# Pairing score units 13 to 20 and issuing one weight load ahead of a cast, in a fused attention and gated-MLP kernel

## Chip, cores and metric

The kernel runs on one core of a Trainium2 chip. The metric is the device time of one execution in microseconds (us). A core has a tensor engine (PE), a vector engine (DVE), a scalar engine (ACT), a Pool engine (POOL) and a sync engine (SP). Each works through its own instruction list in order, and they meet at semaphores. DMA transfers are issued here by SP, ACT and POOL and carried out by 16 DMA engines.

## What is computed

```python
# q: (8, 16, 384, 64)   k, v: (8, 4, 384, 64), each k/v head serves four q heads
scores = scale * np.matmul(q, k.transpose(0, 1, 3, 2))
attn = np.exp(scores - np.max(scores, axis=-1, keepdims=True))
attn = attn / (np.sum(attn, axis=-1, keepdims=True) + 1e-09)
x = np.matmul(attn, v)               # heads side by side: (8, 384, 1024)
h = np.maximum(x @ w_in, 0.0)        # w_in: (1024, 1024)
u, v = h[..., :512], h[..., 512:]
v_n = (v - mean(v)) / np.sqrt(var(v) + 1e-06)
v_s = np.einsum('ts,bsd->btd', w_spatial, v_n) + b_spatial[None, :, None]
out = (u * v_s) @ w_out              # w_out: (512, 1024)
```

## The kernel before

**Work and its pieces.** There are eight batches. The attention of a batch is cut into six sets (three blocks of 128 queries by two groups of heads), and a set into three units, one for each block of 128 keys. So a batch is 18 units and the whole kernel 144. For a unit, `units` (its matmuls on line 278) makes two score tiles of 128x512, called sc, one for each head half (hh 0 and 1); these two matmuls use 64 rows of the array each and start together. `exp` (line 290) turns each into a part of aT on ACT. When the three units of a set are done, `weigh` (line 298) multiplies aT with v, once per head half, in 12 matmuls of 65 columns into av; DVE divides by the row sums (lines 311 and 313) and writes x. `x_turn`, `q_turn` and `k_turn` transpose x, q and k on PE (tiles xps, qps, kps), and DVE copies them out of PSUM (line 216). From the second batch on, x is transposed by DMA (`x_send`, line 337), and from the third on so are k and q (`k_send`, line 248, and `q_send`, line 256).

**The gated part.** `v_part` (line 353) multiplies the transposed x with the v half of w_in, in eight matmuls per block of 128 rows into one PSUM bank (pv). DVE then applies the maximum (line 367) and the statistics (line 379). `u_part` (412), `s_part` (431) and `o_part` (469) make u, the spatial product and the output. A generator, `gated`, hands out these matmuls one by one.

**Order.** The order is written out by hand and is the program's order on every engine. For units 0 to 20 the loop takes one unit at a time: the unit's two scores and its exponentials, then what the table `todo` puts there (casts, transposes, loads), then the halves of `weigh` that are due, then `pour` takes gated matmuls out of the generator until a budget of 736 ns, less 224 for a transpose and 372 for a half of `weigh`, is spent. From unit 21 on the loop takes the three units of a set together, six scores in a row. `bank` gives each PSUM tile one of eight banks by a planner's clock of its own.

**Start.** The v half of w_in comes in two transfers on POOL's queue, `load_w_in(1, 0, 4)` and `load_w_in(1, 4, 8)` (line 161), each 512 rows of 512 float32 columns, cast to float16 on the way. `v_part` needs the first for its matmuls 0 to 3 and the second for 4 to 7. POOL also casts k, v and part of q (lines 185, 189, 206), and SP brings the rest of batch 0's q (`rest_q`, two transfers on line 122). In front of the scores of batch 1 stand `k_turn(1, 0)` at unit 15, `q_turn(1, 0, 0)` at unit 16, `k_turn(1, 1)` and `q_turn(1, 1, 0)` at unit 18; `x_turn` stands at units 5, 9, 12, 15, 18 and 21.

Of the kernel before, what the change touches and what calls it, by code (L numbers as in the profile page):

```python
# [17 lines left out]
def kernel(  # L18
# [58 lines left out]
    def bank(shape, dtype, name):  # L77
        i = min(range(8), key=done.__getitem__)
        t = ps.tile(shape, dtype, name=name, tag=f"bank{i}")
        clock[nc.tensor] = max(clock[nc.tensor], done[i])  # L80
        done[i] = 1e12 + clock[nc.tensor]
        taken[name] = i
        return t

    def spend(ns):
        clock[nc.tensor] += ns

    def reads(eng, ns, name=None):
        clock[eng] = max(clock[eng], clock[nc.tensor] + 200.0) + ns
        if name:  # L90
            done[taken.pop(name)] = clock[eng]
# [67 lines left out]
    def load_w_in(half, lo, hi):  # L159
        cols = slice(half * DH, (half + 1) * DH)  # L160
        pool.dma_start(
            w_in16[:, lo:hi, cols],
            moe_w_in[lo * P : hi * P, cols].rearrange("(t p) f -> p t f", p=P),
        )
# [22 lines left out]
    def cast_v(b, eng, js=(0, 1)):  # L187
        g0, g1 = 2 * js[0], 2 * js[-1] + 2
        eng.tensor_copy(
            v1[b % 2][:, g0:g1, :, 0:D].rearrange("p g t d -> p (g t) d"),  # L190
            stage["v", b, None][:, g0:g1].rearrange("p g (t d) -> p (g t) d", t=NT),
        )

    def cast_q(b, j, eng, ts=None, hs=(0, 1)):
        if (b, j) not in q16s:
            q16s[b, j] = ld.tile([P, NT, G, 2, D], FP16, name=f"q16_{b}_{j}", tag="q16", bufs=4)
        t16 = q16s[b, j]
        src = stage["q", b, j].rearrange("p h t (r d) -> p h t r d", d=D)
        for hh in hs:
            if ts is None:  # L200
                eng.tensor_copy(t16[:, :, :, hh, :], src[:, hh])  # L201
            elif len(ts) > 1:
                t = slice(ts[0], ts[-1] + 1)
                eng.tensor_copy(t16[:, t, :, hh, :], src[:, hh, t])  # L204
            else:
                eng.tensor_copy(t16[:, ts[0], :, hh, :], src[:, hh, ts[0]])
# [57 lines left out]
    def units(u, count):  # L264
        b, r = divmod(u, UNITS)
        s, kt0 = divmod(r, NT)
        qt, j = divmod(s, 2)
        kts = range(kt0, kt0 + count)
        if kt0 == 0:
            aTs[b, s] = att.tile([P, NT, 2, G * P], FP16, name=f"aT_{b}_{s}", tag="aT", bufs=3)  # L270
        scs = [
            (kt, hh, bank([P, G * P], FP32, f"sc_{b}_{s}_{hh}_{kt}"))
            for hh in range(2)
            for kt in kts
        ]
        for kt, hh, sc in sorted(scs, key=lambda x: x[:2]):
            rows = slice(hh * D, (hh + 1) * D)
            nc.tensor.matmul(  # L278
                sc,
                kTs[b][rows, j, kt * P : (kt + 1) * P],  # L280
                qTs[b, j][rows, qt].rearrange("p (r i c) -> p i r c", r=G, i=G),
                start=True,
                stop=True,
            )
        spend(count * C512 + 186)
        return [(aTs[b, s][:, kt, hh], sc, f"sc_{b}_{s}_{hh}_{kt}") for kt, hh, sc in scs]

    def exp(a, sc, name):
        reads(act, 480.0, name)
        act.activation(a, sc, AF.Exp, scale=scale)  # L290

    def weigh(b, s, hh):
        qt, j = divmod(s, 2)
        aT = aTs[b, s]
        av = bank([P, 512], FP32, f"av_{b}_{s}_{hh}")
        for kt in range(NT):
            for i in range(G):
                nc.tensor.matmul(  # L298
                    av[:, i * (D + 1) : (i + 1) * (D + 1)],
                    aT[:, kt, hh, i * P : (i + 1) * P],  # L300
                    v1[b % 2][:, 2 * j + hh, kt, 0 : D + 1],
                    start=(kt == 0 and i == 0),
                    stop=(kt == NT - 1 and i == G - 1),
                )
        if s == 0 and hh == 0:
            x16s[b] = att.tile([P, NT, DM], FP16, name=f"x16_{b}", tag="x16")
        o = av[:, 0 : G * (D + 1)].rearrange("p (i d) -> p i d", i=G)
        spend(372)
        r = small.tile([P, G, 1], FP32, name=f"r_{b}_{s}_{hh}", tag="r")
        reads(dve, 600.0, f"av_{b}_{s}_{hh}")  # L310
        dve.reciprocal(r, o[:, :, D : D + 1])  # L311
        c = j * 512 + hh * 256
        dve.tensor_tensor(  # L313
            x16s[b][:, qt, c : c + 256].rearrange("p (i d) -> p i d", i=G),
            o[:, :, 0:D],
            r.to_broadcast([P, G, D]),
            ALU.mult,
        )
        measure()
# [253 lines left out]
    def idle(count):  # L573
        name = f"idle_{idle_no[0]}"
        ps = bank([P, P], FP32, name)
        done[taken.pop(name)] = clock[nc.tensor] + 400.0
        idle_no[0] += 1
        for _ in range(count):
            nc.tensor.matmul(ps, zero16, zero16, start=True, stop=True)
# [10 lines left out]
    q_turn(0, 0, 0, dve)  # L590
    idle(5)

    cast_v(0, pool, (0,))
    load_w_in(1, 4, 8)
    cast_q(0, 1, pool, (1,))
    cast_v(0, pool, (1,))
    load_k(1, pool)
# [98 lines left out]
    def pour(n, owed):  # L696
        while owed > 0:
            if n < wait_for[0]:
                return 0.0
            x = next(fill, None)  # L700
            if x is None:
                return 0.0
            if isinstance(x, tuple):
                wait_for[0] = x[1]
            else:
                owed -= x
        return owed

    def turn_x(b, s, n):
        if s % 2 and b:  # L710
            x_send(b, s // 2)

    ALONE = 21
    F = (0.2, 0.3, 0.1, 0.4)
    owed = 0.0
    halves = {}
    for u in range(ALONE):
        for pair in units(u, 1):
            exp(*pair)
        spare = 736  # L720
        for f, args in todo.pop(u, []):
            f(*args)
            spare -= 224 if f in (q_turn, x_turn, k_turn) else 0
        for b, s in ends.pop(u, []):
            halves.setdefault(u, []).append((b, s, 0))
            halves.setdefault(u + (0 if s == 0 else 1), []).append((b, s, 1))
        for h in halves.pop(u, []):
            weigh(*h)
            spare -= 372
            if h[2]:  # L730
                turn_x(*h[:2], u)
        owed = pour(u, min(owed, 0) + spare)
# [64 lines left out]
```

## Time and profile before

| what | value |
|---|---|
| three timed runs | 239.06, 239.55, 240.74 us (median 239.55) |
| the profiled execution | 239.07 us, of which the span is 237.0 us |
| granted PE clock | 0.998 |
| busy: PE | 230.4 us (97% of the span) |
| busy: ACT, DVE, POOL | 169.4, 142.9 and 101.4 us (71%, 60%, 43%) |

The span runs from the program's first instruction to its last; 2.07 us of the profiled execution lie outside it. An engine's busy time counts what its instructions took; the ends of matmuls are modelled, so a start-to-start distance between two matmuls says more than the busy time between them. The chain is the work that ended last, followed back from the end; it gives to each piece the time until the next one could go on. "a <- b" means that a is written from b, and an arrow in brackets names what ended an engine's idle time.

### The profile page before, as it was taken

How to read it: one execution, taken by the hardware profiler on the slowest of the kernel's cores; microseconds unless marked ns; L12 is line 12 of the kernel's file. 1: busy time of each engine (PE TensorE's matmuls, PEld its weight loads, DVE VectorE, ACT ScalarE, POOL GpSimd, SP SyncE). 2: the span in 40 equal slices, each digit the busy share in tenths (PEclk: the TensorE clock that was granted, in tenths of full speed). 3: DMA queues.
4: the chain of work that ended last, by engine and by line, in shares of the span. 5: the costliest groups of instructions: out<-in, count | busy, mean ns of one | idle time of the engine just before them, and what ended most of it. 6: DMA issues, size and time to landing. Idle time of an engine off the chain costs nothing.

```text
span 237.0 us, 5921 instructions
## 1 busy us (share of the span) xinstructions
PE 230.4 (97%) x2312; PEld 123.3 (52%) x2312; DVE 142.9 (60%) x379; ACT 169.4 (71%) x348; POOL 101.4 (43%) x145
## 2 busy tenths in 40 slices
PE   6999999999999999999999999999999999999993
PEld 6545565645554445555464445555465455545541
DVE  2668775676447674566645577366744767367362
ACT  2999989969897869978697776986597776401211
POOL 3679583551466442275045800566022500460550
PEclk9999999999999999999999999999999999999999
DMA  6999949999999999997998599929912543240147
GB/s 184 290 321 313 278 116 166 167 321 215 297 226 238 332 300 180 354 205 184 169 309 203 182 207 295 272 88 159 253 27 44 114 147 96 48 177 0 66 200 268
DMA packets 67467, 47.47 MB, mean 200 GB/s; under 512 B 48336, under 2 KB 60416, under 8 KB 67440
## 3 DMA queue, kind: packets, MB, share of 16 engines
q1 hardware_dynamic: 62512, 39.86, 67.7%
q0 software_dynamic: 3952, 6.42, 12.1%
q10 hardware_dynamic: 976, 0.82, 1.1%
q8 instruction: 18, 0.29, 0.5%
q14 instruction: 9, 0.07, 0.1%
HBM read 25.95 MB, written 12.58 MB: 163 GB/s over the span
## 4 chain that ended last, share of the span: by engine, by line
PE 79%; DMA 15%; DVE 1%; POOL 1%; SPq 1%; issue 0%
PE pu L412 17%; PE po L469 16%; PE pv L353 15%; PE sc L278 12%; PE av L298 12%; PE psp L431 6%; DMA xt<-x 4%; DMA w_in<-in_moe_w_in_dram 4%; DMA q<-in_q_dram 3%; DMA v_None<-in_v_dram 2%; DMA qT<-q 2%; POOL vn L397 1%; PE qps L238 1%; DVE osb L216 1%; POOL q L204 0%; SPq L256 0%
## 5 line engine op out<-in xcount | busy, mean ns | idle before, releaser
L290 ACT ACTIVATE aT<-sc 128x512 f16<-128x512 f32 x288 | 147.7, 618 | 31.5 <-PE sc L278 30.5
L298 PEld LDWEIGHTS <-aT 128*128 128x128 f16 x1152 | 47.0, 97 | 16.8 <-issue 2.0
L353 PE MATMUL pv<-w_in,xt 128*128 128x512 f16 x192 | 50.9, 380 | 0.4 <-DMA w_in<-in_moe_w_in_dram 0.2
L298 PE MATMUL av<-v,aT 128*128 128x65 f16 x1152 | 50.5, 193 | 0.0
L469 PE MATMUL po<-w_out,gT 128*128 128x512 f16 (+2 forms) x196 | 50.5, 375 | 0.0
L412 PE MATMUL pu<-xt,w_in 128*128 128x384 f16 x256 | 49.9, 326 | 0.0
L397 POOL TENSOR_SCALAR vn<-vr,rstd,nmr 128x512 f16<-128x512 f32 x23 | 17.7, 783 | 69.9 <-DVE nmr L392 48.5
L448 POOL TENSOR_TENSOR gT<-vs,uT 128x384 f16<-128x384 f32 x31 | 32.5, 1059 | 31.9 <-DVE r L311 16.9
L313 DVE TENSOR_TENSOR x<-av,r 128x256 f16<-128x256 f32 x96 | 40.7, 424 | 3.3
L278 PE MATMUL sc<-qT,kT 64*128 64x512 f16 x288 | 42.3, 380 | 0.5 <-DVE qT L216 0.2
L311 DVE RECIPROCAL r<-av 128x4 f32<-128x4 f32 x96 | 17.1, 178 | 40.8 <-PE av L298 40.5
L216 DVE COPY osb<-po 128x512 f32<-128x512 f32 (+1 forms) x39 | 26.6, 683 | 17.3 <-PE po L469 17.2
L412 PEld LDWEIGHTS <-w_in 128*128 128x128 f16 x256 | 22.1, 98 | 17.1 <-issue 5.5
L423 ACT ACTIVATE uT<-pu 128x384 f16<-128x384 f32 x32 | 15.8, 495 | 16.1 <-PE pu L412 16.0
L469 PEld LDWEIGHTS <-gT 128*128 128x128 f16 x196 | 17.4, 98 | 17.3 <-issue 3.3
L353 PEld LDWEIGHTS <-xt 128*128 128x128 f16 x192 | 15.8, 97 | 18.0 <-issue 5.1
L278 PEld LDWEIGHTS <-kT 64*128 64x128 f16 x288 | 11.0, 94 | 25.4 <-issue 13.8
L431 PE MATMUL psp<-wsT,vn 128*128 128x384 f16 x96 | 22.2, 327 | 0.0
L443 DVE TENSOR_TENSOR vs<-psp,bias_bc 128x384 f32<-128x384 f32 x32 | 17.6, 552 | 7.0 <-PE psp L431 6.9
L367 DVE TENSOR_SCALAR vr<-pv 128x512 f32<-128x512 f32 x24 | 16.4, 682 | 8.4 <-PE pv L353 8.3
L201 POOL CAST q<-q 128x768 f16<-128x768 f32 x22 | 17.7, 833 | 7.8 <-PE av L298 3.0
L379 DVE BATCH_NORM_STATS2 stats<-vr 128x6 f32<-128x512 f32 x24 | 16.4, 685 | 0.1
(47 smaller groups left out, 98.0 us busy)
## 6 DMA issues: line engine op xcount, KB each, us to landing
out_dram<-osb SPq DMA_DIRECT2D x21, 512.0 KB, 2.8
q<-in_q_dram SPq DMA_DIRECT2D x10, 768.0 KB, 7.3
v_None<-in_v_dram SPq DMA_DIRECT2D x6, 384.0 KB, 4.5
w_in<-in_moe_w_in_dram POOLq DMA_DIRECT2D x4, 512.0 KB, 10.4
k_None<-in_k_dram SPq DMA_DIRECT2D x5, 384.0 KB, 3.9
q<-in_q_dram POOLq DMA_DIRECT2D x2, 768.0 KB, 8.7
out_dram<-osb SPq DMA_DIRECT2D x5, 256.0 KB, 2.3
w_out<-in_moe_w_out_dram POOLq DMA_DIRECT2D x2, 512.0 KB, 9.4
```

What stands on the lines that cost most here:

```text
L201: eng.tensor_copy(t16[:, :, :, hh, :], src[:, hh])
L216: (act.copy if eng is act else dve.tensor_copy)(o, i)
L278: nc.tensor.matmul(sc, kTs[b][rows, j, kt * P : (kt + 1) * P], qTs[b, j][rows, qt].rearrange("p (r i c) -> p i r c", r=G, i=G), start=True ...
L290: act.activation(a, sc, AF.Exp, scale=scale)
L298: nc.tensor.matmul(av[:, i * (D + 1) : (i + 1) * (D + 1)], aT[:, kt, hh, i * P : (i + 1) * P], v1[b % 2][:, 2 * j + hh, kt, 0 : D + 1], st ...
L313: dve.tensor_tensor(x16s[b][:, qt, c : c + 256].rearrange("p (i d) -> p i d", i=G), o[:, :, 0:D], r.to_broadcast([P, G, D]), ALU.mult,)
L353: nc.tensor.matmul(pv, xts[b][:, kt, st * P : (st + 1) * P], w_in16[:, kt, DH:DFF], start=(kt == 0), stop=(kt == NK - 1),)
L397: (dve if b == 0 and st == 1 else pool).tensor_scalar(vn, v_r.pop((b, st)), rstd[:, st : st + 1], nmr[:, st : st + 1], op0=ALU.mult, op1=A ...
L412: nc.tensor.matmul(pu[:, 0:S], w_in16[:, kt, m * P : (m + 1) * P], xts[b][:, kt, :], start=(kt == 0), stop=(kt == NK - 1),)
L431: nc.tensor.matmul(psp[:, 0:S], v_n[b, st][:, m * P : (m + 1) * P], wsT16[:, st, :], start=(st == 0), stop=(st == NT - 1),)
L448: pool.tensor_tensor(gT, vs, uT, ALU.mult)
L469: nc.tensor.matmul(po[:, 0:width], gTs[b][:, m, tt * P : (tt + 1) * P], w_out16[:, m, c0 : c0 + width], start=(m == 0), stop=(m == NM - 1),)
```

## The change

Two edits. In the start, POOL issues the second half of the v part of w_in ahead of its first cast of v instead of behind it. In the loop over single units, units 13 and 14, 15 and 16, 17 and 18, and 19 and 20 make their scores and exponentials together, at the first of each two. What else stands at a unit stays at it. The budget that `pour` starts from is 600 at the first unit of two and 870 at the second, in place of 736 at each.

```diff
     q_turn(0, 0, 0, dve)
     idle(5)
 
+    load_w_in(1, 4, 8)
     cast_v(0, pool, (0,))
-    load_w_in(1, 4, 8)
     cast_q(0, 1, pool, (1,))
     cast_v(0, pool, (1,))
...
+    TWO = 13
     for u in range(ALONE):
-        for pair in units(u, 1):
-            exp(*pair)
-        spare = 736
+        if u < TWO or (u - TWO) % 2 == 0:
+            pairs = units(u, 1)
+            if u >= TWO and u + 1 < ALONE:
+                pairs += units(u + 1, 1)
+            for pair in pairs:
+                exp(*pair)
+        spare = 736 if u < TWO else (600 if (u - TWO) % 2 == 0 else 870)
         for f, args in todo.pop(u, []):
             f(*args)
             spare -= 224 if f in (q_turn, x_turn, k_turn) else 0
```

## The prediction, as recorded before the run

> **What bounds the kernel now.** I read the page first, then the chain and the waits of PE over the stretch that the change touches, then the timelines of POOL, ACT and SP there.
>
> ```profile
> span 237.0 us, 5921 instructions
> PE 230.4 (97%) x2312; PEld 123.3 (52%) x2312; DVE 142.9 (60%) x379; ACT 169.4 (71%) x348; POOL 101.4 (43%) x145
> ...
> PE 79%; DMA 15%; DVE 1%; POOL 1%; SPq 1%; issue 0%
> ```
>
> PE is the bound: it is busy nearly all the time, and the chain lies on it for 79%. What PE saves, the kernel saves, as long as no one makes it wait elsewhere. The chain from 16 us on shows what a unit costs on PE (columns: start, us, what), and one piece from 36 us what three units in a row cost:
>
> ```profile
> 7.79 8.40 DMA w_in<-in_moe_w_in_dram
> 16.20 0.04 issue
> 16.24 0.38 PE pv L353
> 16.61 0.32 PE sc L278 x2
> 16.93 0.47 PE av L298 x12
> 17.41 0.43 PE pv L353 x2
> ...
> 22.52 0.33 PE qps L238 x4
> 22.85 0.36 PE av L298 x12
> ...
> 35.98 0.75 PE sc L278 x6
> ```
>
> Two scores take 0.32 us and six take 0.75, so a further pair costs (0.75 - 0.32) / 2 = 0.215, and 0.105 is paid once per group. The av group behind scores takes 0.47, behind a transpose only 0.36: another 0.10, paid by whatever follows a group. Each group that is merged into another therefore saves about 0.20 us of PE. The same rows show the one visible stall of this stretch: PE goes on at 16.24 because the second half of w_in landed at 16.20.
>
> Next ACT, which would have to take the scores faster:
>
> ```profile
> 14.35 7.25 ACT L290 ACTIVATE aT<-sc 128x512 f16<-128x512 f32 x13
> 21.79 3.08 ACT L290 ACTIVATE aT<-sc 128x512 f16<-128x512 f32 x6 [0.20 <-PE sc L278]
> 25.07 4.31 ACT L290 ACTIVATE aT<-sc 128x512 f16<-128x512 f32 x8 [0.20 <-PE sc L278]
> ```
>
> Back to back, the exponentials start every 0.48 us (22 starts from 6.21 to 16.26), so two units need 1.91 us of ACT, while PE spends 2.45 us on two (scores of units 13 and 15 start at 18.86 and 21.31). From 21.6 us on ACT waits for scores. ACT is not the bound in units 13 to 20.
>
> **The change, part one: the pairs.** The order of the built programs shows four merges (units 13 and 14, 15 and 16, 17 and 18, 19 and 20); the number of instructions on each engine stays. Gross: 4 x 0.195 = -0.78 us of PE.
>
> What is handed back I found by walking the new order with starts of the trace, from 18.86 us on (pair 0.22, end of a group 0.10, entry 0.10, av 0.37, one pv 0.215, kps 0.18, xps or qps 0.235). Unit 15's scores then begin at 21.11 instead of 21.31, as one merge should give. Three places wait:
>
> - x_turn at unit 15 needs both halves of set 3. DVE had written the last of it at 21.77 and PE's xps started at 21.81: no slack even before. In the new order the halves stand closer, and between them DVE does reciprocal, product, bn_stats (0.68 us), bn_aggr, reciprocal, product. The last product now ends at about 21.95; xps, which could start at 21.83, starts at 21.99: +0.17.
> - x_turn at unit 18 needs set 4 likewise: product ends at 24.90, xps could start at 24.89: +0.05.
> - The second score behind unit 20 reuses the bank that pv of block 1 held; DVE's line 367 empties it at about 27.61, and PE comes at 27.52: +0.13, in place of +0.15 of small bank waits that the scores from 27.87 to 28.42 show now (0.05 and 0.10 above their usual distance). Net 0.
>
> Other waits are covered: banks of unit 14, 16, 18 and 20 are free by 18.95, 20.37, 23.10 and 25.34, and PE needs them at 19.08, 21.33, 23.36 and 25.48; the q of batch 1 (copy ends 23.18) is needed at 23.36. If ACT or DVE is 0.2 us later than I put it, these covers are gone and each costs about that. Walked to the end, the first av of batch 1 starts at 28.83 instead of 29.38: -0.55. From there on the order of PE differs by one pv matmul within a group and then is the same. I take -0.50 for part one; bounds are -0.78 (none of the waits) and 0 (below).
>
> Does it arrive at the end? PE next waits on others at 55.09, for q of batch 2 (SP's timeline; columns: start, us, issue):
>
> ```profile
> 34.26 1.24 SPq L337 DMA_TRANSPOSE xt<-x  x1
> 35.60 1.63 SPq L248 DMA_TRANSPOSE kT<-k  x1
> 37.33 4.81 SPq L256 DMA_TRANSPOSE qT<-q  x2
> 42.19 0.59 SPq L122 DMA_DIRECT2D q<-in_q_dram  x1
> ```
>
> The first of these is released by x (DVE's product ends at 34.24), so it moves with PE. In the packet records no transfer moves anything from 34 to 35 us, so a start 0.5 earlier finds idle DMA engines, and what SP issues behind it follows: q landed at 48.90, its cast on POOL, its transpose landed at 55.05. I let the 0.5 pass. If the landing stays at 55.05, all of it is lost there.
>
> **Part two: the load.** What POOL does around it:
>
> ```profile
> 6.14 0.50 POOL L185 CAST k<-k_None 128x384 f16<-128x384 f32 x1 [1.59 <-DMA k_None<-in_k_dram]
> 7.34 0.51 POOL L189 CAST v<-v_None 128x384 f16<-128x384 f32 x1 [0.70 <-DMA v_None<-in_v_dram]
> 7.79 0.75 POOL L161 DMA_DIRECT2D w_in<-in_moe_w_in_dram  x1
> 9.43 0.75 POOL L206 CAST q<-q 128x256 f16<-128x256 f32 x2 [0.89 <-DMA q<-in_q_dram]
> ```
>
> The issue (0.75 us) moves to 6.59, into the 0.70 us that POOL waits for v; it ends at 7.34, when v's cast starts anyway. Without that cover the cast would be 0.75 later, and its reader (av at 9.12, cast ends at 7.85) has 1.2 us. The cast of q at 9.43 waits for its own data, so POOL's later issues (k, q, v of batch 1) keep their times.
>
> Does the half land earlier? Packet records of POOL's queue: the first half, issued at 3.60, moves its first packet at 7.5, 3.9 us later; per half microsecond from 10.0 it moves 84, 33, 6, 37, 83 packets of 1 KB, the dip being the end of the first half (landed 12.02) and the start of the second, 3.6 us behind its issue at 7.79. In the dip SP's rest of q takes the engines. The last of 16 rings finished the first half just before 12.02, later than the second half was ready (about 11.4), so on that ring nothing stood idle to be filled, and it is the last ring that sets 16.20. I take 0. Bounds: -0.39 if the stall of PE at 16.24 goes (pv starts 0.39 above its usual distance behind av), and +0.23 if the second half slows the rest of q: its first part landed at 12.80 and DVE casts it at 13.26; 1.1 us later, DVE's next product and PE's xps at 14.57 are 0.62 late, of which the stall at 16.24 takes back 0.39.
>
> By the Trainium skill (DMA: Bandwidth & Descriptors, Queues, rings and completion order) each DMA engine takes the queues that have work in turn, packet by packet, and one queue's descriptors in order; the packet counts agree (from 21 to 26 us the two queues move 44 to 62 and 33 to 54 packets per half microsecond). Against the move speaks the Trainium skill (SBUF — State Buffer, SBUF: two separate sides): POOL cannot write descriptors while DVE runs a float32 copy between SBUF tiles in its two-port mode; by that, DVE's casts at 6.74 to 7.24, which the issue now meets, would hold it up, and the sum would stay within the 1.2 us of cover. The issue at 3.60, beside DVE's cast of 4.03, took 0.94 us against 0.75 for the others.
>
> **Sum.** 239.07 (span 237.0 and 2.07 around it) - 0.78 + 0.17 + 0.05 + 0.06 (rounding to what the walk bears) + 0 = 238.57, say 238.6. The profiled execution lies 0.48 below the median of the runs (239.55) and at their low end, so the median of the new kernel may read some tenths higher.
>
> **Rivals.**
> - A, forecast: pairs give 0.3 to 0.8, the load nothing; 238.3 to 238.8. Chance 0.53.
> - B, the load lands early enough as well: 239.07 - 0.50 - 0.39 = 238.2. For: POOL's queue dips to 6 packets at 11.0. Against: the last ring. Chance 0.15.
> - C, the gain is lost at 55.09, since the landing there hangs on things that do not move: the w_out loads of POOL (34.20, behind a k that landed at 31.79) share the DMA engines from 36 to 44 us. 239.0. Chance 0.18.
> - D, slower: SP's queue between 35 and 50 us. Two q transposes took SP 4.81 us, the first of them 3.49 against 1.23 for the second, because the DMA queue was full. If the earlier xt makes the second one block as well, everything behind it is 3.49 - 1.23 = 2.26 later, q lands at 51.2, and PE waits at 55.09 for as long: 239.07 + 2.26 = 241.3. It decides as soon as the landing passes 55.05. For: that queue already blocks. Against: the idle DMA at 34. Chance 0.10, half of it for a block of a smaller size.
> - E, the pairs do not do what they say, because ACT or a bank holds the second scores back by 0.2 each: 239.1. Chance 0.04.
>
> **Numbers.** Range: from B with none of the waits (239.07 - 0.78 - 0.39 = 237.9), a little lower for the part of a small wait later on, 237.7, to C and E with the spread of the runs (239.06 to 240.74) above them, 240.2. About 1% (2.4 us) is what a measurement of this kernel can tell from no change. No case reaches 1% below; D with a bit more passes it above: faster 0.03, within 1% 0.92, slower 0.05.
>
> **What would show it.** Right: scores of unit 15 at 21.1, four scores 0.22 apart in pairs; PE at the first av of batch 1 0.4 to 0.6 earlier; w_in still landing near 16.2; the wait at 55 moved by the same. Wrong: w_in landing by 15.8 (B); qT of batch 2 still landing at 55.05 with a longer wait of PE (C) or later (D); scores of units 14 to 20 apart by more than 0.3 (E); DVE waiting for q before its cast at 13.26.

## The result, and the profile after

Over 21 runs each, the changed kernel took 240.77 us in the median (238.78 to 244.87), the kernel before 239.23 us (238.37 to 240.74). The ratio is 1.0048, with a 95% interval of 1.003 to 1.0066: slower by about 1.1 us (0.7 to 1.6), where 0.5 us faster had been forecast. (Runs more than 1.5% above the fastest of their kernel, 4 of the 21 of the changed kernel, are left out of ratios, here and below.) The profiled execution took 241.07 us.

The top of the page after:

```profile
span 239.0 us, 5920 instructions
PE 230.9 (97%) x2312; PEld 124.0 (52%) x2312; DVE 142.5 (60%) x379; ACT 169.5 (71%) x348; POOL 101.3 (42%) x145
...
PE 85%; DMA 12%; DVE 1%; ACTq 0%; ACT 0%; issue 0%
```

The engines do the same work; the span is 2.0 us longer, more than the 1.1 us between the kernels, so the steps below explain this one execution. Who PE waited for (the waits of PE after; us in total, times, longest):

```profile
PE xps L330 <- DVE x L313: 1.2, 2, 1.0
...
PE av L298 <- POOL v L189: 0.9, 1, 0.9
PE pv L353 <- DMA xt<-x: 0.5, 1, 0.5
PE sc L278 <- DMA qT<-q: 0.3, 1, 0.3
```

The wait for w_in is gone, and three others took its place. The first is on DVE's timeline after (start, us, instruction, in brackets idle time and what ended it):

```profile
15.16 0.49 DVE L206 CAST q<-q 128x256 f16<-128x256 f32 x2 [1.40 <-DMA q<-in_q_dram]
15.57 0.18 DVE L311 RECIPROCAL r<-av 128x4 f32<-128x4 f32 x1
15.78 0.42 DVE L313 TENSOR_TENSOR x<-av,r 128x256 f16<-128x256 f32 x1
```

DVE stands 1.40 us in front of its cast of the rest of q; behind the cast, in the same list, wait the reciprocal and the product that PE's xps needs. Before, the same cast and product ran without a wait, and PE's xps of unit 9 went through in one piece:

```profile
13.26 0.55 DVE L206 CAST q<-q 128x256 f16<-128x256 f32 x2
...
14.14 0.42 DVE L313 TENSOR_TENSOR x<-av,r 128x256 f16<-128x256 f32 x1
```

```profile
14.57 0.40 PE L330 MATMUL xps<-ident,x 128*128 128x128 f16 x4
14.90 0.39 PE L278 MATMUL sc<-qT,kT 64*128 64x512 f16 x2
```

PE's timeline after, in the same place and a little later:

```profile
14.99 0.28 PE L330 MATMUL xps<-ident,x 128*128 128x128 f16 x2
16.26 0.29 PE L330 MATMUL xps<-ident,x 128*128 128x128 f16 x2 [0.98 <-DVE x L313]
16.48 0.39 PE L278 MATMUL sc<-qT,kT 64*128 64x512 f16 x2
...
20.05 0.61 PE L278 MATMUL sc<-qT,kT 64*128 64x512 f16 x4
...
22.28 0.61 PE L278 MATMUL sc<-qT,kT 64*128 64x512 f16 x4
```

Within xps, start to start, the stall is 1.14 us; by the scores behind it, 1.16. The difference to before along PE's list (start after minus start before):

| PE instruction | before | after | difference |
|---|---|---|---|
| scores of unit 9 | 14.25 | 14.67 | +0.42 |
| scores of unit 10 (behind xps) | 14.90 | 16.48 | +1.58 |
| scores of unit 11 (behind w_in) | 16.55 | 17.73 | +1.19 |
| scores of unit 13 | 18.86 | 20.05 | +1.19 |
| first av of batch 1 | 29.38 | 29.97 | +0.59 |
| second output group of batch 0 | 50.15 | 50.73 | +0.59 |
| first av of batch 2 | 51.05 | 52.64 | +1.59 |
| pv of batch 2, block 2 | 85.33 | 87.34 | +2.02 |
| last output group | 232.89 | 234.89 | +2.01 |

The first 0.42 arises before 9 us, where the k of batch 0 landed at 6.79 instead of 6.08 and the q that releases the rest of q at 7.27 instead of 6.72, so that SP issued the rest of q at 7.84 instead of 7.29. These loads stand ahead of both edits, and from profile to profile the k landed between 5.79 and 7.30, so I put that to chance. The stall at xps costs 1.16, the vanished wait for w_in returns 0.39, the pairs return 0.60, and then 1.00 and 0.43 are lost later.

### The profile page after: what moved, and what is told of

The parts are those of the page before. It is cut to its first block, busy times and chain, and to the rows that moved or that the text cites. A ratio compares the mean times of both kernels' runs of the same rounds, so it can differ in the third digit from the quotient of the medians.

```text
span 239.0 us, 5920 instructions
## 1 busy us (share of the span) xinstructions
PE 230.9 (97%) x2312; PEld 124.0 (52%) x2312; DVE 142.5 (60%) x379; ACT 169.5 (71%) x348; POOL 101.3 (42%) x145
## 4 chain that ended last, share of the span: by engine, by line
PE 85%; DMA 12%; DVE 1%; ACTq 0%; ACT 0%; issue 0%
PE pu L412 18%; PE po L469 17%; PE pv L353 15%; PE sc L278 13%; PE av L298 13%; PE psp L431 7%; DMA q<-in_q_dram 5%; DMA xt<-x 4%; DMA qT<-q 2%; PE qps L238 1%; PE xps L330 1%; DVE osb L216 1%; DVE q L206 0%; DVE x L313 0%; ACTq L122 0%; PE kps L224 0%
## 5 line engine op out<-in xcount | busy, mean ns | idle before, releaser
L278 PE MATMUL sc<-qT,kT 64*128 64x512 f16 x288 | 41.8, 384 | 0.3 <-DMA qT<-q 0.3
```

The source lines that it names most:

```text
L278: nc.tensor.matmul(sc, kTs[b][rows, j, kt * P : (kt + 1) * P], qTs[b, j][rows, qt].rearrange("p (r i c) -> p i r c", r=G, i=G), start=True ...
```

## The experiments

Three theories stood after this. T: the moved load costs, because its packets share the DMA engines with the rest of q. R1: the pairs cost. R2: the profiled run merely started late. Each kernel was compared with the kernel before on the same chip; the kernel before had medians of 239.60 (first four experiments), 239.23 (next four) and 239.32 us (last).

### The pairs alone

```diff
-    load_w_in(1, 4, 8)
     cast_v(0, pool, (0,))
+    load_w_in(1, 4, 8)
```

> The pairs alone, the second half of w_in issued behind the first cast of v as before. Theory T (the moved load is what costs: its packets share the DMA engines with the rest of q, whose first part landed at 15.13 in place of 12.80): 0.4 to 0.7 us faster than the kernel before, 238.6 to 238.9 us, the first rest of q landing at 12.6 to 13.4, PE at the first av of batch 1 about 0.55 ahead of before. Rival R1 (the pairs cost): 240 to 241 us. Rival R2 (chance: the k of batch 0 landed 0.7 late in the profiled run): no difference to before, 239.2 us.

Measured: 238.93 us, ratio 0.9964 (0.9941 to 0.9988): faster by 0.3 to 1.4 us. The first part of the rest of q landed at 12.13, and DVE did not wait for it. From unit 13's scores to the first av of batch 1, PE gained 0.60 against before. At that av it was 1.12 ahead in all: 0.14 came with an earlier start, and 0.39 because w_in's second half landed at 15.59 and was not waited for, though its issue stood in its old place. PE's timeline:

```profile
18.34 0.61 PE L278 MATMUL sc<-qT,kT 64*128 64x512 f16 x4
18.87 0.54 PE L298 MATMUL av<-v,aT 128*128 128x65 f16 x12
...
20.57 0.61 PE L278 MATMUL sc<-qT,kT 64*128 64x512 f16 x4
```

From pair to pair 2.23 us, against 2.45 for two single units before. R1 falls, and so does R2 in its form that the edits make no difference.

### The moved load alone

```diff
+    load_w_in(1, 4, 8)
     cast_v(0, pool, (0,))
-    load_w_in(1, 4, 8)
```

(Against the kernel before; its units stay one at a time.)

> The moved load alone, units one at a time as before. Theory T: slower than the pairs and the load together, 240.8 to 241.4 us; the first rest of q lands at 14.5 or later, DVE waits over 1 us for it, xps of unit 9 stalls by over 0.7 us, and the stall of PE at the second half of w_in is gone. R1 (pairs cost): 239.2 us. R2 (chance): 239.2 us.

Measured: 241.22 us, ratio 1.0068 (1.0031 to 1.0105): slower by 0.7 to 2.5 us. The load is the part that costs. Its profile is of its longest execution (243.67 us), so the order of events counts here and not the size: DVE waited for the rest of q (landed 15.44), then xps for DVE, as after the change.

```profile
15.46 0.49 DVE L206 CAST q<-q 128x256 f16<-128x256 f32 x2 [2.12 <-DMA q<-in_q_dram]
15.87 0.18 DVE L311 RECIPROCAL r<-av 128x4 f32<-128x4 f32 x1
```

### Both parts, with the rest of q released earlier

```diff
+    at(2, rest_q, 0)
+    at(2, rest_q, 1)
     at(2, cast_q, 0, 1, dve, (0,))
-    at(2, rest_q, 0)
-    at(2, rest_q, 1)
```

> The changed kernel with the two tiny memsets that release the rest of q ahead of DVE's cast of q instead of behind it, so that SP issues the rest of q at about 5.9 instead of 7.8. Theory T (the rest of q is late because it shares with the second half of w_in): its packets go ahead of that half, the first part lands by 13.3, DVE does not wait, 238.6 to 239.4 us. R1 and R2: stays at 240.8. A third way: the rest of q now takes the engines from the first half of w_in or from v, and the wait of PE moves to pv at unit 7 (12.5) or to av at 9.1; 239.5 to 240.5.

Measured: 238.64 us, ratio 0.9965 (0.9941 to 0.9989). The moved load is still in, and its loss is gone. SP issued the rest of q at 6.01, its first part landed at 12.71, and DVE ran on:

```profile
13.14 0.42 DVE L313 TENSOR_TENSOR x<-av,r 128x256 f16<-128x256 f32 x1
13.48 0.48 DVE L206 CAST q<-q 128x256 f16<-128x256 f32 x2
14.15 0.18 DVE L311 RECIPROCAL r<-av 128x4 f32<-128x4 f32 x1 [0.19 <-PE av L298]
```

The packet records of the profiles show the mechanism (us; the rest of q is 512 packets on SP's queue, its first part 256 of them; w_in's second half begins with packet 513 of POOL's queue):

| kernel | first packet of w_in's second half | 256th packet of the rest of q | its first part landed | from its issue to its landing |
|---|---|---|---|---|
| before | 11.54 | 11.31 | 12.80 | 5.51 |
| pairs alone | 11.22 | 10.91 | 12.13 | 5.21 |
| after | 10.53 | 13.46 | 15.13 | 7.29 |
| load alone | 10.36 | 13.25 | 15.44 | 8.01 |
| w_out early (below) | 10.25 | 12.96 | 14.76 | 7.98 |
| rest of q earlier (this one) | 10.70 | 11.52 | 12.71 | 6.70 |

Where the load kept its old place, POOL's queue falls to 5 or 6 packets per half microsecond near 11 us, and the first part of the rest of q goes through that gap. Where the second half is ready as the first ends, there is no gap, and the two queues share: from 11.5 to 14.0 after the change, POOL's queue moved 69, 64, 62, 60 and 51 packets per half microsecond and SP's 48, 55, 59, 54 and 68. With the early release, the rest of q has its head start by another way (first packet at 9.68 instead of 10.50).

### Both parts, with the w_out loads earlier on POOL

```diff
+    at(20, load_w_out, 0, DH)
+    at(20, load_w_out, DH, DM)
     at(20, cast_k, 2, pool)
...
-    at(26, load_w_out, 0, DH)
-    at(26, load_w_out, DH, DM)
```

> The changed kernel with the two loads of w_out ahead of POOL's casts of batch 2's k and q instead of behind them, about 2.3 us earlier on POOL. If the second loss (PE waits 1.05 us at av of batch 2 at 52.6, for v of batch 2, cast at 51.76) comes from POOL being 1.4 late and w_out loads then sharing the DMA engines with the transposes and loads of batch 2: that wait shrinks to under 0.4 and the time to 239.8 to 240.2. If it comes from SP's own order or from later x: the wait stays near 1.0 and the time at 240.8.

This asks for the second loss, at 52.64 after. PE's timeline after, then POOL's:

```profile
50.73 1.03 PE L469 MATMUL po<-w_out,gT 128*128 128x512 f16 x4
52.64 0.52 PE L298 MATMUL av<-v,aT 128*128 128x65 f16 x12 [0.88 <-POOL v L189]
```

```profile
35.64 1.50 POOL L167 DMA_DIRECT2D w_out<-in_moe_w_out_dram  x2
...
50.54 1.17 POOL L204 CAST q<-q 128x512 f16<-128x512 f32 x2 [2.23 <-DMA q<-in_q_dram]
51.76 0.83 POOL L189 CAST v<-v_None 128x768 f16<-128x768 f32 x1
```

Measured: a median of 241.65 us over twelve runs, six of them between 238.99 and 240.01 and six between 243.28 and 250.05; ratio 0.9995 (0.9967 to 1.0024). In the profiled execution (239.66 us) w_out is issued at 32.47, its second half lands at 42.32 instead of 48.37, and PE's wait at that av is 0.16 instead of 1.05:

```profile
32.47 1.50 POOL L167 DMA_DIRECT2D w_out<-in_moe_w_out_dram  x2
...
49.53 1.17 POOL L204 CAST q<-q 128x512 f16<-128x512 f32 x2 [1.34 <-DMA q<-in_q_dram]
50.76 0.83 POOL L189 CAST v<-v_None 128x768 f16<-128x768 f32 x1
```

So that wait hangs on when the w_out loads run, as expected. The packet records agree: after the change, w_out moved 120 to 150 packets per microsecond from 40 to 45 us, and the transposes beside it 93 to 158; with w_out earlier its last packet went at 41.74 us, and the transposes moved 946 packets in the microsecond from 42. The q of batch 2, issued behind them, then took 4.31 us to land instead of 7.59. As a cure the edit is not usable, since half of its runs are longer than any of the kernel before. What those runs wait for was not seen, and stays open. The landing of w_out does not settle the time of v's cast alone: with the loads in their old place it landed at 44.17 (pairs alone), 46.08 (before), 47.60 (load still later, below) and 48.37 (after), and the cast of batch 2's v ended at 49.60, 51.00, 52.03 and 52.59; but here it landed at 42.32 with the cast ending at 51.58, since the transposes met w_out earlier and SP issued that q at 45.17 instead of 42.89. This profile also has a loss of its own: PE waited 1.36 us at 12.71 for a part of q (see the last experiment), and xps of unit 9 only 0.21.

### The pairs, with the w_out loads earlier

The edit of the last experiment, on the pairs alone.

> The pairs without the moved load, and the two w_out loads ahead of POOL's casts of batch 2's k and q. With POOL on time there is no wait of 1.05 us at av of batch 2 to remove; the wait at the scores near 54 us (0.9 us in the pairs alone) may shrink. Theory: 0 to 0.5 us below the pairs alone, 238.4 to 238.9. Rival: moving w_out ahead makes the k and q of batch 2 late instead, and runs scatter above 242 as they did with the moved load.

Measured: 238.45 us (ten runs, 237.98 to 239.66), ratio 0.9957 (0.9927 to 0.9987). The scatter above 242 did not come. The interval lies nearly on that of the pairs alone, and from the av ahead of the scores near 54 us to the pv behind them PE took 1.92 us as there, as before and as after (about 0.8 of it waiting), so a gain over the pairs is not shown.

### The pairs, with the rest of q released earlier

The edit of the third experiment, on the pairs alone.

> The pairs and the early release of the rest of q, the load of w_in where it was before. If the moved load, once the rest of q is out of its way, is worth nothing: the same as with it, 238.5 to 238.9. If it was worth the 0.39 us wait at pv of unit 10: 238.9 to 239.2. Theory: the first.

Measured: 238.82 us, ratio 0.9973 (0.9945 to 1.0000). Within the intervals this is the same with the moved load (0.9965) and without: the move is worth nothing that can be measured, even where it does no harm. Its profile shows why: w_in's second half, issued in its old place, landed at 16.13 and PE did not wait for it. Nor did it in the pairs alone (15.59) or in the pairs with w_out earlier (15.70). The wait of 0.39 that the move was to remove is in the profile before, but not in every execution.

### The pairs, with the load later still

```diff
     cast_v(0, pool, (0,))
-    load_w_in(1, 4, 8)
     cast_q(0, 1, pool, (1,))
+    load_w_in(1, 4, 8)
     cast_v(0, pool, (1,))
```

> The pairs, with the second half of w_in issued later still, behind POOL's cast of q at about 10.1 in place of 7.8. Theory T (sharing): the rest of q has the engines to itself and lands by 12.5, DVE does not wait; the half of w_in lands near 18, and PE waits 1.5 to 2 us at pv of unit 10: 240.2 to 240.9. Rival (its place in the queue does not matter, since one ring ends last anyway): 238.9.

Measured: 240.46 us, ratio 1.0029 (0.9999 to 1.0059). The rest of q landed at 12.33 and 13.04 (before: 12.80 and 15.00), the half of w_in at 17.01, and PE waited for it:

```profile
15.80 0.53 PE L298 MATMUL av<-v,aT 128*128 128x65 f16 x12
17.05 0.38 PE L353 MATMUL pv<-w_in,xt 128*128 128x512 f16 x1 [0.72 <-DMA w_in<-in_moe_w_in_dram]
```

Issued 2.4 us later than before, the half landed only 0.8 later, and the second part of the rest of q 2.0 earlier. Start to start the wait is 0.89, half of what I expected; another 0.85 follows at the av of batch 2. The rival falls: the place in the queue matters. It does so by deciding which of two loads has the engines first.

### The pairs from unit 9 on

```diff
-    TWO = 13
+    TWO = 9
```

> The pairs alone, but from unit 9 on: six merges in place of four. If a merge is worth its two changes of tile (0.195 us) wherever it stands: 0.4 us below the pairs alone, 238.5. If ACT, which runs back to back up to 16 us, or the late x of a set holds PE there: no gain or a loss, 238.9 to 239.3. Theory: the second, since scores cannot be taken faster than ACT empties the banks there.

Measured: 239.81 us, ratio 1.0009 (0.9974 to 1.0043): the gain of the pairs alone is not seen, as expected, but mainly by other waits than the one on ACT that I gave as the reason. PE waited 0.62 for w_in at 17.21 and 0.35 for x in the middle of an xps, the late x that I had named beside ACT; the four scores at 15.08 took 0.15 longer than those at 17.74:

```profile
16.23 0.53 PE L298 MATMUL av<-v,aT 128*128 128x65 f16 x12
17.21 0.59 PE L353 MATMUL pv<-w_in,xt 128*128 128x512 f16 x2 [0.45 <-DMA w_in<-in_moe_w_in_dram]
...
19.09 0.28 PE L330 MATMUL xps<-ident,x 128*128 128x128 f16 x2
19.55 0.29 PE L330 MATMUL xps<-ident,x 128*128 128x128 f16 x2 [0.19 <-DVE x L313]
```

In this profile the k of batch 0 landed late too (7.30), so how much of the first wait belongs to the edit is open.

### A combination

The pairs, the load in its old place, the early release of the rest of q, and the early w_out loads.

> A candidate for the best version: the pairs, the load of w_in where it was, the early release of the rest of q, and the w_out loads ahead of POOL's casts of batch 2. If the three act on different waits: 238.0 to 238.5, below the pairs alone. If what the last two remove is no longer waited for once the pairs run without the moved load: the same as the pairs alone, 238.4 to 238.9. I expect the second, with fewer runs above 239.5.

Measured: 240.50 us (239.03 to 241.54), ratio 1.0043 (1.0018 to 1.0068): slower than the kernel before, against both expectations. In its profile the part of q that ACT brings for unit 6 landed at 12.84 instead of 9.38, and PE waited 1.41 us for its transposes at 13.69. Each of the two edits without the other kept the gain of the pairs, but the late part is not special to the combination. In the four profiles in which w_in's first half moved its first packet at 6.50 to 6.63, this part landed at 10.65 to 12.84; in the other seven, with a first packet at 6.67 to 7.64, it landed at 9.22 to 9.93. Three of the four are the kernels with the early w_out loads (PE lost 1.36, 0.40 and 1.41 us there), the fourth is the pairs from unit 9 on. Whether those loads, which run 20 us later, have a part in that order or it is chance is open. The best versions that ran are, not told apart by their intervals, the pairs alone, the pairs with one of the two edits, and the changed kernel with the early release.

## Why the prediction was wrong, by its steps

**The pairs: right.** The walk through the new order gave -0.55 at the first av of batch 1. It was -0.60 there after the change, in the pairs alone, and with the early release, with and without the moved load, each counted from unit 13's scores. So the walk was 0.05 short, and the term of -0.50 by 0.1. The pairs alone measured 0.3 to 1.4 us faster, which holds the forecast's 0.3 to 0.8. What the walk handed back to xps of unit 15 as 0.17 was 0.09; at unit 21 an xps, which the walk had not looked at, waited 0.31, and the scores behind it waited that much less.

**The load's issue: no cost, as predicted, but not by the cover that I named.** It was to end as v landed. POOL's timeline after:

```profile
6.85 0.50 POOL L185 CAST k<-k_None 128x384 f16<-128x384 f32 x1 [2.30 <-DMA k_None<-in_k_dram]
7.29 0.80 POOL L161 DMA_DIRECT2D w_in<-in_moe_w_in_dram  x1
8.09 0.52 POOL L189 CAST v<-v_None 128x384 f16<-128x384 f32 x1
```

With k late, POOL began the issue only 0.22 us ahead of v's landing (7.51), and the cast ran 0.58 us behind that landing: about 0.5 us lost on POOL, inside the second cover of 1.2, so PE did not wait. The port rule of the Trainium skill (SBUF — State Buffer, SBUF: two separate sides) that I set against the move did not decide: the issue took 0.80 us beside DVE's casts from 7.30, against 0.75 before.

**The load's landing: right.** 16.41 after the change, 16.20 before: the half came no earlier for being issued earlier.

**The rest of q: the step that failed.** I had this as a bound, "+0.23 if the second half slows the rest of q", and took 0. The place was right: the first part late, DVE's cast late, xps of unit 9 late, the wait for w_in taken back; and DVE's wait for q, which I had named as a sign of being wrong, came with 1.40 us. The size was not. I let the two loads share for little more than the 1.2 us by which the issue moved, and put the first part 1.1 us late. They share until the second half is through, from 10.5 to about 14.5. The first part landed 2.33 late; 0.55 of that is its later issue, and the other 1.78 its longer way (7.29 us in place of 5.51). Xps stalled 1.16, and the net in the profile is 1.16 - 0.39 = +0.77 in place of the bound's +0.23 and of the 0 in the sum. The same queue rule that I quoted from the Trainium skill (DMA: Bandwidth & Descriptors, Queues, rings and completion order: an engine serves the queues that have work in turn) gives this; the packet counts above agree with it. (The first of the two ranges that I gave for 21 to 26 us should be 48 to 63 packets, not 44 to 62.) I had written that SP's rest of q takes the engines in the gap of POOL's queue, and still put nothing in the sum for what it loses when the gap is filled.

**What hangs on POOL behind it: not in the sum.** I wrote that POOL's later issues (k, q, v of batch 1) keep their times. These did, but for 0.28 us of the late start, and I looked no further. POOL's cast of the second part of the rest of q went from 15.13 to 17.01, and with it everything behind it in POOL's list: the w_out loads went from 34.20 to 35.64. They then ran beside the transposes and loads of batch 2 for longer, and batch 2's v was cast 1.6 us later. Before, that cast stood here:

```profile
50.17 0.83 POOL L189 CAST v<-v_None 128x768 f16<-128x768 f32 x1
```

**Where PE next waits: wrong.** I named the scores at 55.09. The first av of batch 2 was closer: before, v's cast ended at 51.00 and PE began that av at 51.05. With no slack, it took 1.00 of the loss. The third wait, at 87.34 for x of batch 3, follows at 0.43; no experiment took it by itself. In the pairs alone it was under 0.1.

**The rivals.** B is refuted by the landing, E by the 0.60. C did not come in the pairs alone: PE was 1.12 ahead at the first av of batch 1 and 1.16 ahead at the first av of batches 2 and 3. D had the sign, but another cause: it needed an earlier xt on SP's queue and put q 2.26 late, while the xt came 0.66 later and q was issued 0.70 later. What was late were POOL's and DVE's lists behind one load. That an issue on SP lengthens while an earlier transpose is unmoved, on which D rested, shows elsewhere: with w_out earlier, the transpose wsT had moved nothing when SP issued the first xt at 34.73, and that issue took 3.99 us against 1.24 before.

## What to carry to other kernels

A gap in one DMA queue may be what lets another queue's load through in time: before a load is issued earlier, list every load in flight in the time that it will now occupy, and what waits behind each in its consumer's list. When queues share, count the sharing until one of the loads ends, not for the time by which the issue moved. And look for the next point of no slack on every engine that is made late, not only on the engine that is the bound.

## What the runs showed of the hardware that I had not expected

Two queues of different kind shared the DMA engines at nearly one packet each (62 to 59 from 12.5 to 13.0), though a packet of w_in is read as 2 KB of float32 and one of the rest of q as 1 KB. And the start varies: the k of batch 0, issued at about 1.65 in every profile, landed between 5.79 and 7.30, and the scores of unit 6 began between 10.78 and 11.98, a spread of twice what the pairs gain.
